# Routed attention and cosine-routed experts: one late block instead of two, a first wide item of 392 rooms placed right behind the early blocks and turned by TensorE, and the overflow branch moved into the last early result

## The chip, the cores and the metric

One core of a Trainium2 chip runs the whole program. The metric is the device time of one execution in microseconds (us); lower is better. The profile describes one execution by itself, measured from its first to its last instruction (the span).

## What is computed

An attention whose queries see only the keys of their own cluster is followed by a mixture of experts with one expert for each token. Cut to the part that the change touches:

```
def _moe_ref(x, expert_emb, tau, w1, w2):          # x: (3072, 512), E = 8, F = 1024
    ...
    expert_idx = np.argmax(logits, axis=1)         # one expert for each token
    ...
    for e in range(E):
        mask = expert_idx == e
        h = np.maximum(x[mask] @ w1[e], 0.0)       # w1[e]: 512 x 1024
        out[mask] = gate_w[mask, None] * (h @ w2[e])   # w2[e]: 1024 x 512
```

All of it is in float32. Which tokens go to which expert is known only while the program runs, so the kernel gives the experts rooms of fixed sizes and fills them.

## The kernel before

The first 330 us or so are the attention. They end in `x_rows`, a DRAM tensor with one row of 512 numbers for each token. After that the expert work is cut into *items*, each with an expert and a number of rooms for tokens. An item has a hidden stage (its rows times `w1`, then the positive part) and a result stage (times `w2`, then the gate), and its output rows are scattered to `out`. There are four kinds.

- Four *early* items of 128 rooms (`E0`), filled from the first half of the tokens while attention still runs.
- *Block* items of 128 rooms (`KX` of them, two before). They take what does not fit the wide items. The first block stood right behind the early items, the other is `last` at the very end.
- Eight *sized* items, called wide here, one for each expert, with the rooms of `CAPS`. The experts are ranked by what is left for them and get the rooms in that order. All but the smallest are multiplied by a scheme with seven products in place of eight: `sized_hidden` and `sized_result` cut rows and weights into quarters and call `seven`, which keeps partial sums. A wide item has 2 x 28 matmuls in its hidden stage and 56 in its result, each as wide as half its rooms. VectorE makes the sums of `x` (`x_sums`), of `w1` (`w1_sums`), of the hidden rows (`h_sums`) and of `w2` (`w2_sum`); ScalarE copies parts of `w2` (`w2_copy`). The smallest (200 rooms) uses `plain_hidden` and `plain_result`.
- *Whole* items of 128 rooms that stand inside `overflow()`, a branch (`tc.If`) taken only if more blocks are used than `KX`.

Five engines run their own lists, written out by hand (`tc.manual_schedule`), so the order of the calls in the code is the order on each engine. Weight loads, and the transfers of rows between DRAM and the chip's memory, are issued by SP in that order. GpSimd (POOL) issues the gathers of rows by index (`collect`) and the scatters to `out`. There are two buffers for `w1` (`w1s`) and two for `w2` (`w2s`). Wide items load their raw `w2` into one buffer (`slot2`), and their sums and copies fill the other one and some tiles beside it.

The rows of a block or wide item take a detour before: `collect` gathers them, `lay` writes them to the DRAM tensor `x_slots`, `bring` reads them back in another layout (`xs`, `xin`), and `turn_x` turns them on VectorE by 32 x 32 transposes into `xT`, with the model dimension on the partitions.

The order around the change was: hidden of the early item `E0[3]`, result of `E0[2]`, result of `E0[3]`, hidden of the first block, the matmuls that sort gates into slots (`pb.gates`), result of the block, the matmuls that spread these gates (`spread_gates`), and then the wide items from the largest to the smallest. The overflow branch stood between `plain_hidden` and `plain_result` of the last wide item. At the branch every engine loads the number of used blocks (`used`), compares and jumps. Where the paths meet, each engine waits for its own work: PE, VectorE and ScalarE for their instructions, POOL also for its transfers, SP for its own transfers. Later instructions that use a buffer which the branch could have used wait for the engine concerned to have come past that place.

Of the kernel before, what the change touches and what calls it, by code (L numbers as in the profile page):

```python
# [9 lines left out]
F32 = mybir.dt.float32  # L10
# [8 lines left out]
P = 128  # L19

SQ = 32
# [18 lines left out]
def kernel(  # L40
# [12 lines left out]
    nc = tc.nc  # L53
# [18 lines left out]

    CAPS = (344, 344, 336, 328, 280, 264, 248, 200)
    KX = 2
    assert len(CAPS) == E and max(CAPS) <= 512
# [6 lines left out]

    MORE = (2, 6, 12)
    NO = sum(MORE)
# [1134 lines left out]
    def collect(it):  # L1219

        to = mo.setdefault(it, {})["rows_in"] = []
        for i, (b, n) in enumerate(rows_of(it)):
            if it is sized[0]:
                x = szp.tile(
                    [P, FH, HC], F32, tag=("h11", "h12", "h21")[i], name="rows_in", bufs=1
                )
# [15 lines left out]
    def bring(it):  # L1242

        d = mo[it]
        if it.kind == "sized":
            to, n = szp.tile([P, max(WIDE), P], F32, tag="xs", name="xs", bufs=1), WIDE[it.j]
            d["xs"] = to
        else:
            to, n = xip.tile([P, NQ, P], F32, tag="xin", name="xin"), NQ
            d["xin"] = to  # L1250
        for w in range(NQ):
            nc.sync.dma_start(
                out=to[SQ * w : SQ * w + SQ, 0:n], in_=by_quads(x_slots, it, n)[w]
            )
# [26 lines left out]
    def turn_x(it, evict=None, xT=None):  # L1281
# [25 lines left out]
        evict(d["xT"], bk)  # L1307

    HC = max(CAPS) // 2
    KH = KD // 2  # L1310
# [41 lines left out]
    def w2_part(it, name):  # L1352

        parts = mo[it].setdefault("w2", {})
        if name not in parts:
            own = ("t2", "t4", "b21", "b22")
            if name in own:
                i = own.index(name)
                t = flat(w2s[0][:, 2 * i : 2 * i + 2]).rearrange("p (g f x) -> p g f x", g=2, f=FH)
# [40 lines left out]
    def seven(it, product, to, relu, then):  # L1400
# [6 lines left out]

        def saved(name, src):
            t = szp.tile([P, 2, HC], F32, tag=name, name=name, bufs=1)[:, :, 0:h]
            nc.scalar.copy(t, src)  # L1410
            return t
# [181 lines left out]
    def hidden(it, halves=(0, 1), span=(0, 512)):  # L1593

        d = mo[it]
        for half in halves:
            if half == 0 and span[0] == 0:
                d["hT"] = mop.tile([P, F], F32, tag="hT", name="hT")
            f0 = 512 * half
# [34 lines left out]

    def result(it, halves=(0, 1)):
        d = mo[it]
        for half in halves:
# [6 lines left out]
            bk = d["y_ps"]  # L1644
            for c in range(KF // 2 * half, KF // 2 * half + KF // 2):
                nc.tensor.matmul(  # L1646
# [5 lines left out]
                )  # L1652
            if half == 1:
                to = (sidxs[0] if it.kind == "early" else it.tables[2])[:, it.col : it.col + 1]
# [49 lines left out]
    YB = 1  # L1704
    kinds = 4 * "early " + "block " + E * "sized " + "block"
    items = []
    for i, kind in enumerate(kinds.split()):
        own = 1 if i > KA else i % 2
        items.append(Item(kind, sum(it.kind == kind for it in items), i % 2, own))
# [4 lines left out]
    later = items[KA:]  # L1714
    sized = later[1:-1]

# [69 lines left out]
    with tc.manual_schedule(engines=by_hand):  # L1786
# [96 lines left out]
        pb.experts()  # L1883
        weights1(later[0])
        result(E0[1], (0,))
# [9 lines left out]
        pb.token_rows(gidxs[1], sidxs[1])  # L1895
        collect(later[0])
        collect(sized[0])
# [18 lines left out]
        weights2(sized[0])  # L1916
        collect(sized[1])

        def overflow():
            n_used = nc.values_load(used[0:1, 0:1], min_val=0, max_val=KX + NO)  # L1920
            own = sized[-1]

            def more(j0, n):
                for j in range(j0, j0 + n):
                    it = Item("whole", KX + j, own.slot, own.slot2, more_tables)
                    it.col, it.gates, it.xin = j, more_gates, xin
# [8 lines left out]
            with tc.If(n_used > KX):  # L1935
# [3 lines left out]
                ]  # L1939
                xin = szp.tile([P, max(WIDE), P], F32, tag="xs", name="xs", bufs=1)[:, 0:NQ]  # L1940
                pb.hot_blocks(NB, NO)
# [22 lines left out]

# [66 lines left out]
        plain_hidden(it, steps)  # L2031
        overflow()
        weights2(last)
# [50 lines left out]
```

## Time and profile before

| | us |
|---|---|
| median of 3 runs (lowest to highest) | 658.21 (658.02 to 660.22) |
| the profiled execution's own time | 656.26 |
| its span, first to last instruction | 654.5 |
| PE busy in the span | 638.2 (98%) |
| VectorE (DVE) busy | 488.3 (75%) |
| ScalarE (ACT) busy | 315.4 (48%) |
| POOL busy | 177.6 (27%) |
| granted TensorE clock, mean | 0.996 |

PE is TensorE's matmul stream and PEld its weight loads, which lie beside it. In rows of the time line the columns are: start and duration in us from the span's start, engine, line of the kernel, operation, output<-input by the program's names, shape, and the number of equal instructions merged; in brackets stands the idle time of that engine just before, and what ended it. A float32 matmul stands as two records, so "x8" there is four matmuls of the code. A transpose by TensorE is one record.

### The profile page before, as it was taken

To read this page: it belongs to the slowest core of one execution; us is meant where nothing else is said; L and a number is where in the kernel's file an instruction comes from. 1 tells how busy PE (TensorE), PEld (TensorE's weight loads), DVE (VectorE), ACT (ScalarE), POOL (GpSimd) and SP (SyncE) were. 2 spreads that over 40 slices of the span, in tenths; PEclk is the share of its full clock that TensorE was granted. 3 is DMA by queue.
4 is the path that set the end of the run, shared out by engine and by line. 5 is a ranking of instruction groups with operands and counts; after the bars stand their busy time and mean duration, and the time that the engine had idled before them with its cause. 6 is when DMAs were issued, how large, how long until landed. Compare 5 with 4: busy or idle time off the path is not lost. (4 is left out here: it accounts for less than half of the span.)

```text
span 654.5 us, 16780 instructions
## 1 busy us (share of the span) xinstructions
PE 638.2 (98%) x6673; PEld 449.0 (69%) x6673; DVE 488.3 (75%) x806; ACT 315.4 (48%) x537; POOL 177.6 (27%) x382
## 2 busy tenths in 40 slices
PE   8999999999999999999999978999999999999996
PEld 4444444444444444445677655999999999999995
DVE  6988988998989999999768234677778778886220
ACT  6656655677655785667615201525252424434311
POOL 3222212312214112235756431220404040220211
PEclk9999999999999999999999989999999999999999
DMA  9855666777679778668989989886969687888753
GB/s 143 134 93 99 98 97 106 141 148 128 96 94 166 132 156 180 109 177 215 273 234 336 374 309 333 230 244 200 291 225 293 233 292 257 278 271 292 266 195 98
DMA packets 261537, 131.47 MB, mean 201 GB/s; under 512 B 208561, under 2 KB 229297, under 8 KB 261452
## 3 DMA queue, kind: packets, MB, share of 16 engines
q1 hardware_dynamic: 256876, 117.36, 71.2%
q0 software_dynamic: 4400, 12.92, 6.3%
q8 instruction: 54, 0.88, 0.6%
q14 instruction: 31, 0.25, 0.1%
q10 hardware_dynamic: 176, 0.05, 0.0%
HBM read 101.18 MB, written 23.54 MB: 191 GB/s over the span
## 5 line engine op out<-in xcount | busy, mean ns | idle before, releaser
L585 ACT ACTIVATE prob<-s_ps 128x768 f32<-128x768 f32 x192 | 154.3, 813 | 100.5 <-PE s_ps L574 98.8
L574 PE MATMUL s_ps<-qT,kT 64*64 64x384 f32 x1536 | 156.1, 483 | 0.0
L596 PE MATMUL o_ps<-prob,v 64*64 64x385 f32 x1536 | 141.2, 484 | 0.0
L615 DVE TENSOR_TENSOR acc<-acc,prob 128x768 f32<-128x768 f32 x128 | 121.4, 948 | 8.6
L596 PEld LDWEIGHTS o_ps<-prob,v 64*64 64x64 f32 x1536 | 57.4, 133 | 65.7 <-issue 58.1
L574 PEld LDWEIGHTS s_ps<-qT,kT 64*64 64x64 f32 x1536 | 55.1, 133 | 36.1 <-issue 31.9
L1141 POOL DMA_INDIRECT out_dram<-rows_out,sidx x22 | 22.9, 1039 | 158.9 <-DMA rows_out<-y_slots 154.9
L574 PE MATMUL s_ps<-hot 64*64 64x384 bf16 x768 | 64.4, 325 | 0.1
L574 PEld LDWEIGHTS <-hot 64*64 64x64 bf16 x768 | 23.9, 106 | 42.8 <-issue 40.6
L630 POOL COPY behind<-acc 1x1 f32<-1x1 f32 x30 | 6.7, 222 | 158.7 <-DVE acc L615 154.3
L1605 PEld LDWEIGHTS h_ps<-xTm,w1s 128*128 128x128 f32 x384 | 45.3, 198 | 6.4 <-issue 6.4
L1605 PE MATMUL h_ps<-xTm,w1s 128*128 128x128 f32 x384 | 46.0, 282 | 3.4 <-issue 3.4
L663 POOL COPY inv<-inv 32x12 f32<-32x12 f32 x128 | 33.0, 258 | 41.7 <-DVE inv L660 33.5
L1646 PE MATMUL y_ps<-w2s,hT 128*128 128x512 f32 x80 | 35.6, 595 | 4.4 <-DMA w2s<-in_moe_w_dram 4.4
L1130 POOL DMA_INDIRECT rows_in<-x_rows,gidx x24 | 29.0, 1207 | 21.5 <-DMA x_slots<-rows_in 16.3
L605 DVE SCALAR_TENSOR_TENSOR acc<-prob,prob 128x768 f32<-128x768 f32 x32 | 32.4, 1013 | 0.0
L1564 DVE STREAM_TRANSPOSE ys<-yT 128x352 f32<-128x352 f32 (+3 forms) x32 | 13.2, 469 | 23.2 <-ACT yT L1440 13.7
L1297 DVE STREAM_TRANSPOSE xTm<-xin 128x512 f32<-128x512 f32 x5 | 3.6, 711 | 36.2 <-DMA xin<-x_slots 19.1
L620 ACT COPY o_sb<-o_ps 128x770 f32<-128x770 f32 x32 | 25.6, 799 | 9.5 <-PE o_ps L596 9.5
L1646 PEld LDWEIGHTS y_ps<-w2s,hT 128*128 128x128 f32 x80 | 14.7, 190 | 21.6 <-issue 19.2
L632 POOL TENSOR_TENSOR o_sum<-o_sb 128x385 f32<-128x385 f32 x30 | 26.5, 884 | 1.4 <-ACT o_sb L620 0.9
L1410 ACT COPY u<-h_ps 128x344 f32<-128x344 f32 (+5 forms) x22 | 9.1, 413 | 33.4 <-PE h_ps L1503 21.6
(351 smaller groups left out, 1129.7 us busy)
## 6 DMA issues: line engine op xcount, KB each, us to landing
w1s<-in_moe_w_dram SPq DMA_DIRECT2D x12, 2048.0 KB, 9.4
w2s<-in_moe_w_dram SPq DMA_DIRECT2D x12, 2048.0 KB, 8.6
q<-in_q_dram SPq DMA_DIRECT2D x64, 96.0 KB, 4.1
k<-in_k_dram SPq DMA_DIRECT2D x64, 96.0 KB, 3.3
x_rows<-xb SPq DMA_DIRECT2D x64, 96.0 KB, 2.7
v<-in_v_dram SPq DMA_DIRECT2D x120, 48.0 KB, 2.0
xr<-x_rows SPq DMA_DIRECT2D x9, 512.0 KB
x_slots<-rows_in SPq DMA_DIRECT2D x17, 256.0 KB, 11.2
```

Source lines behind the costliest of these rows:

```text
L574: nc.tensor.matmul(s_ps[D * half : D * half + D, h, 0:HS], lhsT=l[rows, half], rhs=r[rows], start=part == (1 if len(parts) < 2 else 0), st ...
L585: nc.scalar.activation(d["prob"][:, :, 0:HS], d["s_ps"][:, :, 0:HS], ACTF.Exp, scale=scale)
L596: nc.tensor.matmul(g["o_ps"][D * h : D * h + D, half, 0:HE], lhsT=ld[n]["v"][keys, j, h], rhs=d["prob"][keys, h, 0:HE], start=(j == 0), st ...
L605: nc.vector.scalar_tensor_tensor(out=g["acc"], in0=un[i - 1]["prob"][:, :, 0:HS], scalar=NJ * EPS, in1=d["prob"][:, :, 0:HS], op0=ALU.add, ...
L615: nc.vector.tensor_tensor(g["acc"], g["acc"], d["prob"][:, :, 0:HS], ALU.add)
L620: nc.scalar.copy(t["o_sb"], g["o_ps"][:, :, 0:HE])
L632: add(t["o_sum"][:, hq], t["o_sb"][:, 0], t["o_sb"][:, 1], ALU.add)
L663: nc.gpsimd.tensor_copy(inv2[M * to : M * to + M, :, i % 2], inv[M * i : M * i + M])
L1130: nc.gpsimd.indirect_dma_start(out=to, out_offset=None, in_=of, in_offset=bass.IndirectOffsetOnAxis(ap=at, axis=0), bounds_check=n - 1, oo ...
L1141: inst = nc.gpsimd.indirect_dma_start(out=to, out_offset=bass.IndirectOffsetOnAxis(ap=at, axis=0), in_=of, in_offset=None, bounds_check=n - 1,
L1605: nc.tensor.matmul(bk[:, m : m + P], lhsT=w1s[it.slot][:, c, f0 + m : f0 + m + P], rhs=d["xT"][:, P * c : P * c + P], start=(c == 0), stop ...
L1646: nc.tensor.matmul(bk, lhsT=d["hT"][:, P * c : P * c + P], rhs=w2s[it.slot2][:, c], start=(c == 0), stop=(c == KF - 1),)
```

## The change

The rooms become 392, 344, 344, 336, 328, 280, 248, 200: the size 264 goes and 392 is new. One block is left (`last`). The first wide item comes right behind the early items. Its gathered rows no longer go through DRAM: `order_rows` copies them on VectorE into another order, `turn_rows` turns them by TensorE, and ScalarE and VectorE copy the turned rows to `xT`. The overflow branch stands between the second and third quarter of the result of `E0[3]`; all weight buffers swap their parity; the two saved tiles `u2` and `u3` share one buffer; a few tiles used by whole items are other ones.

```
-    CAPS = (344, 344, 336, 328, 280, 264, 248, 200)
-    KX = 2
+    CAPS = (392, 344, 344, 336, 328, 280, 248, 200)
+    KX = 1
...
-    MORE = (2, 6, 12)
+    MORE = (2, 6, 13)
...
+    def order_rows(it):
...
+            nc.vector.tensor_copy(
+                to.rearrange("p (c w i) -> p c w i", c=KD, w=NQ),
+                x.rearrange("p (w c i) -> p c w i", c=KD, w=NQ),
+            )
...
+    def turn_rows(it):
...
+            for c in range(KD):
+                nc.tensor.transpose(bk[:, c], x[:, P * c : P * c + P], ident[0:n, 0:n])
+            evict = nc.scalar.copy if i % 2 == 0 else nc.vector.tensor_copy
+            evict(d["xT"][:, :, P * i : P * i + n], bk)
...
         def saved(name, src):
+            name = "u2" if name == "u3" else name
...
-    def result(it, halves=(0, 1)):
+    def result(it, halves=(0, 1), parts=2):
...
-    kinds = 4 * "early " + "block " + E * "sized " + "block"
+    kinds = 4 * "early " + E * "sized " + "block"
...
-        own = 1 if i > KA else i % 2
+        own = 0 if i >= KA else i % 2
...
-        weights1(later[0])
+        weights1(sized[0])
...
-        collect(later[0])
         collect(sized[0])
...
-        weights1(sized[0])
-        lay(later[0])
-        lay(sized[0])
-        bring(later[0])
+        w1_sums(sized[0])
         result(E0[2])
-        weights2(later[0])
-        bring(sized[0])
-        turn_x(later[0])
-        w1_sums(sized[0])
-        turn_x(sized[0])
-        result(E0[3])
-        weights2(sized[0])
-        collect(sized[1])
+        order_rows(sized[0])
+        pb.gates(slot_gates)
...
-        first, last = later[0], later[-1]
-        hidden(first)
+        result(E0[3], (0, 1), 4)
+        overflow()
+        weights2(sized[0])
+        weights1(sized[1])
+        collect(sized[1])
+        lay(sized[1])
+        bring(sized[1])
+        result(E0[3], (2,), 4)
+        turn_rows(sized[0])
+        result(E0[3], (3,), 4)
+        spread_gates()
         x_sums(sized[0])
-        pb.gates(slot_gates)
-        lay(sized[1])
-        weights1(sized[1])
-        bring(sized[1])
-        result(first, (0,))
         w2_sum(sized[0], "t1")
-        result(first, (1,))
-        spread_gates()
...
         plain_hidden(it, steps)
-        overflow()
         weights2(last)
```

How the instructions stand on the engines shows where things went. First TensorE, before, from the hidden stage of `E0[3]` on (`w1s_59`, `w1s_58` and `w2s_60`, `w2s_61` are the two buffers of each weight; 48 rows of gates are left out at the first "...", 31 of their spreading at the second):

```order
L1605 MATMUL h_ps<-xTm,w1s_59 128x128 x32
L1646 MATMUL y_ps_5085<-w2s_60,hT 128x512 x8
L1646 MATMUL y_ps_5193<-w2s_61,hT 128x512 x8
L1605 MATMUL h_ps<-xTm,w1s_58 128x128 x32
L1072 LDWEIGHTS ohrb
...
L1646 MATMUL y_ps_5085<-w2s_60,hT 128x512 x8
L1578 LDWEIGHTS identb
...
L1467 MATMUL h_ps<-xTs,w1s_59 128x172 x4
```

And TensorE of the changed kernel at the same place, from the end of the gates on; what stands inside the branch is left out at the first "...":

```order
L1072 MATMUL misc_236<-rg24b,ohrb 128x72
L1686 MATMUL y_ps_5193<-w2s_61,hT 128x512 x4
L1950 TENSOR_LOAD used
L1965 COMPARE_AND_BRANCH
...
L1965 UNCONDITIONAL_BRANCH
L1686 MATMUL y_ps_5193<-w2s_61,hT 128x512 x2
L1340 MATMUL x_ps<-ident,ordered 128x128 x4
L1340 MATMUL h_ps<-ident,ordered 128x128 x8
L1340 MATMUL h_ps<-ident,ordered 128x32 x4
L1686 MATMUL y_ps_5193<-w2s_61,hT 128x512 x2
L1614 LDWEIGHTS identb
...
L1503 MATMUL h_ps<-xTs,w1s_58 128x196 x4
```

The 32 and 8 matmuls of the first block are gone; the gates moved ahead of the result of `E0[3]`, which is cut into pieces of four, two and two matmuls with the branch and 16 transposes between them, and the wide item follows at once.

SP, whose list is also the order in which the transfers are issued, before, from the weights of the first block on:

```order
L1180 DMA w1s_58<-in_moe_w_dram 128x4x1024
L1180 ISA
L1180 DMA w2s_61<-in_moe_w_dram 128x8x512
L1165 TENSOR_LOAD e_sized
L1165 ISA x2
...
L1180 DMA w1s_59<-in_moe_w_dram 128x4x1024
L1235 DMA x_slots<-rows_in 128x512 x3
L1235 DMA x_slots<-rows_in 96x512
L1252 DMA xin<-x_slots 32x4x128 x4
```

And SP of the changed kernel from there, with the inside of the branch left out:

```order
L1180 DMA w2s_61<-in_moe_w_dram 128x8x512
L1950 TENSOR_LOAD used
L1950 ISA x2
L1965 COMPARE_AND_BRANCH
...
L1965 UNCONDITIONAL_BRANCH
L1180 ISA
L1180 DMA w2s_60<-in_moe_w_dram 128x8x512
L1165 TENSOR_LOAD e_sized
...
L1180 DMA w1s_59<-in_moe_w_dram 128x4x1024
L1235 DMA x_slots<-rows_in 128x512 x2
```

The rows of the first wide item no longer pass through SP; its `w2` is the first transfer behind the branch, and `w1s_59`, `x_slots` there are of the second wide item.

More of the change, by code (lines that the diff above doesn't have):

```diff
@@ L1224, in collect @@
                 x = szp.tile(
-                    [P, FH, HC], F32, tag=("h11", "h12", "h21")[i], name="rows_in", bufs=1
+                    [P, FH, HC], F32, tag=("h11", "h12", "h21", "h22")[i], name="rows_in", bufs=1
                 )
@@ L1245, in bring @@
         if it.kind == "sized":
-            to, n = szp.tile([P, max(WIDE), P], F32, tag="xs", name="xs", bufs=1), WIDE[it.j]
+            to, n = szp.tile([P, max(WIDE[1:]), P], F32, tag="xs", name="xs", bufs=1), WIDE[it.j]
             d["xs"] = to
@@ L1307, in turn_x @@
         evict(d["xT"], bk)
+    def order_rows(it):
+        d = mo[it]
+        spare = szp.tile([P, max(WIDE), P], F32, tag="ys", name="ordered", bufs=YB)
+        spare = spare.rearrange("p u x -> p (u x)")
+        d["ordered"] = []
+        for i, (x, _) in enumerate(d.pop("rows_in")):
+            n = x.shape[0]
+            if DM * i + DM <= spare.shape[1]:
+                to = spare[0:n, DM * i : DM * i + DM]
+            else:
+                to = szp.tile([P, FH, HC], F32, tag="hS1", name="ordered", bufs=1)
+                to = to.rearrange("p f t -> p (f t)")[0:n, 0:DM]
+            nc.vector.tensor_copy(
+                to.rearrange("p (c w i) -> p c w i", c=KD, w=NQ),
+                x.rearrange("p (w c i) -> p c w i", c=KD, w=NQ),
+            )
+            d["ordered"].append(to)
+    def turn_rows(it):
+        d = mo[it]
+        d["xT"] = szp.tile([P, KD, SQ * max(WIDE)], F32, tag="xTs", name="xTs", bufs=1)
+        for i, x in enumerate(d.pop("ordered")):
+            n = x.shape[0]
+            if i == 0:
+                bk = psX.tile([P, DM], F32, tag="x_ps", name="x_ps")
+            else:
+                bk = psH.tile([P, 512], F32, tag="h_ps", name="h_ps")
+            bk = bk.rearrange("p (c t) -> p c t", c=KD)[:, :, 0:n]
+            for c in range(KD):
+                nc.tensor.transpose(bk[:, c], x[:, P * c : P * c + P], ident[0:n, 0:n])
+            evict = nc.scalar.copy if i % 2 == 0 else nc.vector.tensor_copy
+            evict(d["xT"][:, :, P * i : P * i + n], bk)
     HC = max(CAPS) // 2
@@ L1358, in w2_part @@
                 i = own.index(name)
-                t = flat(w2s[0][:, 2 * i : 2 * i + 2]).rearrange("p (g f x) -> p g f x", g=2, f=FH)
+                t = flat(w2s[1][:, 2 * i : 2 * i + 2]).rearrange("p (g f x) -> p g f x", g=2, f=FH)
             else:
@@ L1597, in hidden @@
             if half == 0 and span[0] == 0:
-                d["hT"] = mop.tile([P, F], F32, tag="hT", name="hT")
+                if it.kind == "whole":
+                    t = szp.tile([P, KD, SQ * max(WIDE)], F32, tag="yT", name="hT", bufs=1)
+                    d["hT"] = t.rearrange("p g t -> p (g t)")[:, 0:F]
+                else:
+                    d["hT"] = mop.tile([P, F], F32, tag="hT", name="hT")
             f0 = 512 * half
@@ L1644, in result @@
             bk = d["y_ps"]
-            for c in range(KF // 2 * half, KF // 2 * half + KF // 2):
+            for c in range(KF // parts * half, KF // parts * half + KF // parts):
                 nc.tensor.matmul(
@@ L1652, in result @@
                 )
-            if half == 1:
+            if half == parts - 1:
                 to = (sidxs[0] if it.kind == "early" else it.tables[2])[:, it.col : it.col + 1]
@@ L1714 @@
     later = items[KA:]
-    sized = later[1:-1]
+    sized, last = later[:-1], later[-1]
     def piece(n, name, *args):
@@ L1939, in overflow @@
                 ]
-                xin = szp.tile([P, max(WIDE), P], F32, tag="xs", name="xs", bufs=1)[:, 0:NQ]
+                xin = szp.tile([P, max(WIDE[1:]), P], F32, tag="xs", name="xs", bufs=1)[:, 0:NQ]
                 pb.hot_blocks(NB, NO)
```

4 lines of the change are left out of this document (2 added, 2 removed).

## The prediction

> **What bounds the kernel now.** I read the page's busy times first, then the time line of TensorE (PE) behind the attention, then who waits there.
>
> ```profile
> PE 638.2 (98%) x6673; PEld 449.0 (69%) x6673; DVE 488.3 (75%) x806; ACT 315.4 (48%) x537; POOL 177.6 (27%) x382
> 550.00:560.00 10.00, 10.00 (x87) 10.00 (x86) 9.79 (x15) 1.43 (x4) 3.58 (x5) 1.00 0.90 316
> ```
>
> PE is the bound: busy 98% of the span, and all 10 us of the second row, a stretch of 10 us inside the wide items where VectorE (third pair) is nearly full too. So an edit is worth what it takes off PE's line. PE's gaps lie where the early items hand over to the wide ones:
>
> ```profile
> 358.97 7.31 PE L1605 MATMUL h_ps<-xTm,w1s 128*128 128x128 f32 x64
> 366.11 7.03 PE L1646 MATMUL y_ps<-w2s,hT 128*128 128x512 f32 x16
> 374.69 7.10 PE L1646 MATMUL y_ps<-w2s,hT 128*128 128x512 f32 x16 [1.55 <-DMA w2s<-in_moe_w_dram]
> 385.22 9.01 PE L1605 MATMUL h_ps<-xTm,w1s 128*128 128x128 f32 x64 [3.42 <-issue]
> 394.07 0.94 PE L1072 MATMUL misc<-rg24b,ohrb 128*128 128x72 bf16 x24
> 397.87 7.10 PE L1646 MATMUL y_ps<-w2s,hT 128*128 128x512 f32 x16 [2.86 <-DMA w2s<-in_moe_w_dram]
> 405.33 0.30 PE L1578 MATMUL misc<-g3b,identb 128*32 128x66 bf16 x16 [0.36 <-DVE g3b L1082]
> 405.56 1.43 PE L1467 MATMUL h_ps<-xTs,w1s 128*128 128x172 f32 x8
> 406.83 1.33 PE L1467 MATMUL h_ps<-xS,w1s 128*128 128x172 f32 x8
> 408.00 1.33 PE L1467 MATMUL h_ps<-xS,t 128*128 128x172 f32 x8
> ```
>
> In order: hidden of `E0[3]`, result of `E0[2]`, result of `E0[3]`, hidden of the first block, gates, the block's result, spreading, and the first products of the first wide item. From 373.14 (366.11 + 7.03) to 405.56 are 32.42 us. Four gaps of 1.55, 3.42, 2.86 and 0.36 lie in them, and the block's hidden stage takes 9.01 where the same 64 records took 7.31. The long gap comes from the rows' way through DRAM:
>
> ```profile
> 384.40 0.71 DVE L1297 STREAM_TRANSPOSE xTm<-xin 128x512 f32<-128x512 f32 x1 [19.07 <-DMA xin<-x_slots]
> 401.42 1.76 DVE L1288 STREAM_TRANSPOSE xTs<-xs 128x512 f32<-128x512 f32 x3 [11.35 <-DMA xs<-x_slots]
> ```
>
> **The change, part by part.** I sum against the profiled execution (656.26 us by its own time, 654.5 in its span, so 1.76 around it). The median shown is 658.21, 1.95 above it; I take the sum off both.
>
> *The wide item of 392 for that of 264.*
>
> ```profile
> 561.05 1.06 PE L1467 MATMUL y_ps<-xTs,w1s 128*128 128x132 f32 x8
> 586.67 1.05 PE L1467 MATMUL h_ps<-xTs,w1s 128*128 128x124 f32 x8
> 627.06 1.52 PE L1545 MATMUL y_ps<-h,w2b 128*128 128x200 f32 x8
> 628.41 1.52 PE L1545 MATMUL y_ps<-h,w2s 128*128 128x200 f32 x8
> ```
>
> The item of 264 (132 columns) held PE from 561.05 to 586.67, 25.6 us. An item has 112 matmuls. At 172 columns four take 408.00 - 406.83 = 1.17, 0.292 each; at 200 columns 1.35, 0.338. Between them 196 gives 0.332 and the item 37.2 us: **+11.5**. The block's 40 matmuls go in the next part.
>
> *The stretch from 373.14 to the wide item.* What it holds afterwards:
> (a) Gates, 0.94, while the `w2` of `E0[3]` still lands. It was issued at 359.16 (row below) and landed by 374.69; one of the four row gathers beside it shrinks from 128 or 96 rows to 32, so I take 374.3: 1.2 us (bounds 0.9 and 1.6).
> (b) The result of `E0[3]`, in pieces: 7.1.
> (c) The branch, inside it.
>
> ```profile
> 612.22 10.99 PE L1527 MATMUL h_ps<-xTs,w1s 128*128 128x200 f32 x64
> 359.16 0.37 SPq L1180 DMA_DIRECT2D w2s<-in_moe_w_dram  x1
> 624.28 1.59 PE L1545 MATMUL y_ps<-h,w2b 128*128 128x200 f32 x8 [1.06 <-ACTq L1935]
> L1920 PEldq TENSOR_LOAD <-used x1: 487/487/487, 620.0 to 620.0; - x1
> L1935 PEldq COMPARE_BRANCH  x1: 3492/3492/3492, 620.6 to 620.6; - x1
> L1935 DVEq COMPARE_BRANCH  x1: 72/72/72, 614.9 to 614.9; - x1
> ```
>
> PE's jump took 3.49 us, and its sequencer got to it some 2.6 us before the last matmul ended (612.22 + 10.99), so 1.06 us of it showed as a gap. In the new place the sequencer can't run ahead by more than the four matmuls behind the wait for `w2` (3.5 us), less issuing them and the load of `used` (0.49): I estimate it at the jump by 375.6, past it by 379.2, while the array is done by 377.8. That is a gap of 1.4; bounds 0 (hidden) and 3.6 (wholly exposed). [...]
> (d) Sixteen transposes.
>
> ```profile
> L1304 PE MATMUL x_ps<-ident,rows x4: 272/273/328, 318.1 to 318.5; 128*128 128x128 f32 x4
> ```
>
> Four start within 0.4 us, some 0.11 apart: 1.8; the upper bound is 16 x 0.273 = 4.4. The copies of `order_rows` hide: VectorE idled for 19.07 us there, and the last rows had landed when SP sent them on, by 373.3:
>
> ```profile
> 368.45 4.83 SPq L1235 DMA_DIRECT2D x_slots<-rows_in  x4
> ```
>
> They end before 377. The copies to `xT` lie beside (b)'s last piece, 1.8 us.
> (e) Spreading, 0.3.
> (f) A new order on VectorE: the spread gates come ahead of `x_sums`.
>
> ```profile
> 403.22 0.52 DVE L1322 TENSOR_TENSOR xS<-xTs 128x344 f32<-128x344 f32 x1
> 407.57 0.64 DVE L1586 COPY parts<-misc 128x264 f32<-128x264 f32 x1
> 408.70 1.22 DVE L1384 TENSOR_TENSOR w2t<-w2s 128x1024 f32<-128x1024 f32 x1
> ```
>
> The gates take 408.70 - 407.57 = 1.13, the first sum 0.52 x 392/344 = 0.6; the second product needs it, and the first covers 4 x 0.332 = 1.3. With 0.2 for signals PE waits 0.6 (bounds 0 and 1.5).
> Together 1.2 + 7.1 + 1.4 + 1.8 + 0.3 + 0.6 = 12.4 in place of 32.42: **-20.0**. The half clock of the block's hidden stage and all four gaps go with it.
>
> *What is late next: the wide item's `w2`.* SP issues it behind the branch, into a buffer that the branch could have used, so not before PE is past it (379.3).
>
> ```profile
> DMA to landing us min/median/max: 8.3/8.6/9.8
> 407.38 1.05 ACT L1388 COPY w2b<-w2s 128x1024 f32<-128x1024 f32 x1
> ```
>
> That is the time to land of `w2` behind 400 us: 8.6, so 388.1. ScalarE's first copy of it stands between saving the first product (386.3) and the second (388.2), and the third bank is free only behind that. It ends at 389.2, the save at 389.6, and the fourth product would like to start at 389.6. **+0.4**; bounds 0 and 3 (landing in 9.8, with the gathers of the second wide item beside it, and a longer jump).
>
> *Other queues.* POOL meets the branch with a scatter in flight:
>
> ```profile
> 374.14 1.03 POOL L1141 DMA_INDIRECT out_dram<-y,sidx  x1 [7.25 <-ACT y L1657]
> L1935 POOLq COMPARE_BRANCH  x1: 58/58/58, 629.9 to 629.9; - x1
> L1935 POOLq INC_SWDGE_SEM  x1: 1508/1508/1508, 637.2 to 637.2; - x1
> ```
>
> It was held from 629.9 to 638.7 before, 8.8 us; from 375.9 that gives 384.7. Then come the gathers of the second wide item, `lay` and `bring`.
>
> ```profile
> 384.11 1.04 POOL L1130 DMA_INDIRECT rows_in<-x_rows,gidx  x1 [0.31 <-DMA xin<-x_slots]
> 408.38 2.00 SPq L1252 DMA_DIRECT2D xs<-x_slots  x4
> xs<-x_slots SPq DMA_DIRECT2D x12, 176.0 KB, 8.2
> ```
>
> Before, they took 24.3 us from the first gather to `bring`, with two weight loads queued between, and 8.2 to land. These loads now go first; taking one of them (8.6) off, the rows are there by 384.7 + 24.3 - 8.6 + 8.2 = 408.6. VectorE wants them behind the wide item's hidden stage (18.6 from 385.5), its first result product (2.7), four sums of 0.6 and four of 1.2 as above: about 414. Nothing shows, by 5 us.
>
> *`u2` and `u3` in one tile*: ScalarE's save of product 7 now waits for VectorE's sum from `u2`.
>
> ```profile
> 539.24 0.39 ACT L1410 COPY u<-h_ps 128x280 f32<-128x280 f32 x1 [0.69 <-PE h_ps L1467]
> 539.31 0.44 DVE L1427 TENSOR_TENSOR h<-h_ps,u 128x280 f32<-128x280 f32 x1
> ```
>
> This is the tightest of the 21 places: the sum ends at 539.75, so the save slips by 0.5, and one product in between (0.95) covers most of it. **+0.3**; bounds 0 and 1.
>
> *The branch gone from the end*: its 1.06 gap, **-1.1**; PE's last matmuls (below) and the scatter follow as they did.
>
> ```profile
> 642.32 7.11 PE L1623 MATMUL y_ps<-w2s,hT 128*128 128x384 f32 x32
> ```
>
> Sum: 11.5 - 20.0 + 0.4 + 0.3 - 1.1 = **-8.9 us**. Own time 656.26 - 8.9 = 647.4; from the median 658.21 - 8.9 = **649.3**.
>
> **The rivals.**
> *Forecast*, 649.3, own range 647.5 to 651. For it: PE full to 10.00 of 10 once the wide items run, so that its records are all that counts.
> *A new wait takes the old one's place*: the jump ends late, `w2` lands late, ScalarE holds the banks, or the second item's rows miss their 414. For it: each link starts from the one before, at transfer times that reach 9.8. Against: each is a microsecond or two. +3: 652.3.
> *The clock drops.* The block's 9.01 came behind a gap of 3.42, while the gap of 2.86 left the 7.10 behind it alone. If the jump is wholly exposed (3.6, or 2.2 more than I count), the same loss of 1.7 follows: +3.9, 653.2. [...]
> *Less is exposed*: jump hidden, no waits; -1.4 - 0.6 - 0.4 - 0.3 = 646.6.
> *Slower*: POOL at the branch. ScalarE's gating of the result of `E0[3]` reuses an output tile that the branch could scatter from, so it waits for POOL to have come past, and the banks of the wide item queue behind it on ScalarE. It has until 385; every microsecond beyond stops PE for one. POOL's 8.8 us give 384.7, so it just holds. To be slower by 0.5% POOL would have to hold until 397, 21 us at the branch, with the scatter's landing alone 12 us later than before; some 662. A small case of it is in the second rival.
> *The change doesn't do what it says*: if two blocks were used, the branch would run. By the reference's routing 462, 388, 339, 337, 325, 277, 241 and 191 tokens are left for the wide items. 388 fit into 392 with four to spare, as they did into 264 + 128; 462 need 336 + 126, as before, where the branch was skipped. I exclude it.
>
> **How the numbers follow.** Forecast 0.60, new wait 0.17, clock 0.08, less exposed 0.06, waits and clock together (within 0.5%, about 656) 0.05, slower 0.04. Half a per cent, 3.3 us, is about what a measurement of this kernel can tell from no change; faster starts below 654.9. The first four give 0.91 faster, then 0.05 and 0.04. The low end, 646.5, is the fourth case; the high end, 653.5, takes in the third. That leaves out the last two cases and the tails, under 0.2.
>
> **What would show it.** Right: wide item's first matmul at 385 (+-1.5) in PE's time line, its 112 matmuls at 0.332, no row gap on VectorE behind 384, PE without a gap between the plain item's stages, a gap of 1 to 2 us inside the result of `E0[3]`. Wrong: gaps with ScalarE as releaser among the first seven products (`w2` or POOL), half clock behind 378, or a wait of VectorE for `xs`.

## The result, and the profile after

| | before | after |
|---|---|---|
| median of 6 runs (lowest to highest), us | 659.22 (657.51 to 660.89) | 648.41 (648.14 to 649.09) |
| the profiled execution's own time | 656.26 | 648.23 |
| its span | 654.5 | 646.4 |

The ratio is 0.9836, with a 95% interval of 0.9815 to 0.9858: faster by 1.6%. The prediction was 649.3 with a range of 646.5 to 653.5. In the profiled spans the change is worth 8.1 us; the prediction's sum was 8.9. The medians are 10.8 apart because the runs of before lie 1 to 5 us above its one profiled execution, while those of after lie at it. What the other executions of before spent that time on was not traced; the 34 of them that ran beside the kernels below had a granted clock of 0.991 to 0.997, where the changed kernel ran at 0.997 to 1.0.

The page's busy times afterwards:

```profile
PE 635.8 (98%) x6609; PEld 450.9 (70%) x6609; DVE 494.3 (76%) x808; ACT 316.7 (49%) x536; POOL 177.1 (27%) x382
```

TensorE's time line afterwards, over the same stretch as before (columns as before; the last three rows are the start of the second wide item and of the two stages of the smallest one):

```profile
366.56 7.03 PE L1686 MATMUL y_ps<-w2s,hT 128*128 128x512 f32 x16
...
374.54 3.67 PE L1686 MATMUL y_ps<-w2s,hT 128*128 128x512 f32 x8 [0.17 <-SPq L1965]
379.09 1.96 PE L1686 MATMUL y_ps<-w2s,hT 128*128 128x512 f32 x4 [0.87 <-PEq L1965]
380.88 0.60 PE L1340 MATMUL x_ps<-ident,ordered 128*128 128x128 f32 x4
...
382.64 1.98 PE L1686 MATMUL y_ps<-w2s,hT 128*128 128x512 f32 x4
...
384.80 1.59 PE L1503 MATMUL h_ps<-xTs,w1s 128*128 128x196 f32 x8
386.88 1.56 PE L1503 MATMUL h_ps<-xS,w1s 128*128 128x196 f32 x8 [0.48 <-DVE xS L1357]
388.28 1.49 PE L1503 MATMUL h_ps<-xS,t 128*128 128x196 f32 x8
391.01 1.59 PE L1503 MATMUL h_ps<-xS,w1s 128*128 128x196 f32 x8 [1.24 <-ACT p L1446]
...
424.28 1.33 PE L1503 MATMUL y_ps<-xTs,w1s 128*128 128x172 f32 x8
...
605.50 11.00 PE L1563 MATMUL h_ps<-xTs,w1s 128*128 128x200 f32 x64
616.33 1.52 PE L1581 MATMUL y_ps<-h,w2b 128*128 128x200 f32 x8
```

The first wide product starts 11.21 behind the end of the result of `E0[2]` (384.80 - 373.59), where it took 32.42 before. The gaps of 1.55, 3.42 and 2.86 are gone, and so is the 1.06 between the last wide item's stages. In their place stand three smaller ones: 0.87 at the branch (released by PE's own queue at the branch's line), 0.48 for the first sum of `x`, 1.24 in front of the fourth product. That last one names ScalarE's save `p` as the releaser. ScalarE's time line tells why the save was late:

```profile
384.71 0.69 ACT L1697 ACTIVATE y<-y_ps,gatein 128x512 f32<-128x512 f32 x1 [1.74 <-PE y_ps L1686]
386.43 0.48 ACT L1446 COPY p<-h_ps 128x392 f32<-128x392 f32 x1 [1.03 <-PE h_ps L1503]
389.52 1.04 ACT L1423 COPY w2b<-w2s 128x1024 f32<-128x1024 f32 x1 [2.61 <-DMA w2s<-in_moe_w_dram]
390.48 0.48 ACT L1446 COPY p<-h_ps 128x392 f32<-128x392 f32 x1
```

The copy of `w2` stands in ScalarE's list ahead of the second save, and it waited for the load until 389.5. The load itself was issued late, behind the branch. The rows of the branch, and then of the load's issue (line, engine's queue, operation, count: least/median/most ns, first and last start in us):

```profile
L1965 POOLq COMPARE_BRANCH  x1: 58/58/58, 374.9 to 374.9; - x1
L1965 PEldq COMPARE_BRANCH  x1: 3752/3752/3752, 375.2 to 375.2; - x1
```

```profile
L1180 SPq DMA_DIRECT2D w2s<-in_moe_w_dram x1: 397/397/397, 379.1 to 379.1; - x1
```

So the new critical thread is: jump of TensorE until 378.95, `w2` issued at 379.1, landed at 389.5, copied, second save, bank free (the piece of memory that a product is written to), fourth product.

### The profile page after: what moved, and what is told of

Read it like the earlier page. It is cut to its first block, busy times and chain, and to the rows that moved or that the text cites. A ratio compares the mean times of both kernels' runs of the same rounds, so it can differ in the third digit from the quotient of the medians.

```text
span 646.4 us, 16585 instructions
## 1 busy us (share of the span) xinstructions
PE 635.8 (98%) x6609; PEld 450.9 (70%) x6609; DVE 494.3 (76%) x808; ACT 316.7 (49%) x536; POOL 177.1 (27%) x382
## 5 line engine op out<-in xcount | busy, mean ns | idle before, releaser
L1141 POOL DMA_INDIRECT out_dram<-rows_out,sidx x23 | 24.7, 1073 | 166.4 <-DMA rows_out<-y_slots 163.0
L1645 PEld LDWEIGHTS h_ps<-xTm,w1s 128*128 128x128 f32 x320 | 36.4, 192 | 2.2 <-issue 2.2
L1600 DVE STREAM_TRANSPOSE ys<-yT 128x352 f32<-128x352 f32 (+4 forms) x32 | 13.8, 486 | 30.5 <-ACT yT L1588 17.1
L1645 PE MATMUL h_ps<-xTm,w1s 128*128 128x128 f32 x320 | 37.0, 276 | 0.0
L1130 POOL DMA_INDIRECT rows_in<-x_rows,gidx x24 | 27.5, 1146 | 28.7 <-DMA x_slots<-rows_in 23.9
L1686 PE MATMUL y_ps<-w2s,hT 128*128 128x512 f32 x64 | 29.0, 598 | 1.0 <-PEq L1965 0.9
L1446 ACT COPY u<-y_ps 128x344 f32<-128x344 f32 (+5 forms) x20 | 8.6, 428 | 32.0 <-PE y_ps L1539 15.3
L1451 ACT ACTIVATE h<-h 128x344 f32<-128x344 f32 (+5 forms) x42 | 19.7, 475 | 4.5 <-DVE h L1468 2.6
```

The costliest lines, as they stand in the source:

```text
L1130: nc.gpsimd.indirect_dma_start(out=to, out_offset=None, in_=of, in_offset=bass.IndirectOffsetOnAxis(ap=at, axis=0), bounds_check=n - 1, oo ...
L1645: nc.tensor.matmul(bk[:, m : m + P], lhsT=w1s[it.slot][:, c, f0 + m : f0 + m + P], rhs=d["xT"][:, P * c : P * c + P], start=(c == 0), stop ...
L1686: nc.tensor.matmul(bk, lhsT=d["hT"][:, P * c : P * c + P], rhs=w2s[it.slot2][:, c], start=(c == 0), stop=(c == KF - 1),)
```

## Experiments

Each kernel is the changed one with the edit shown, timed in 5 rounds; "..." marks lines of the code that are left out. Spans are of one profiled execution. As executions do not all start the expert stage at the same time (the result of `E0[2]` starts between 365.7 and 368.5), distances are counted from the start of that result where it matters.

| label | median, us | ratio to before [95%] | span |
|---|---|---|---|
| (the change) | 648.41 | 0.9836 [0.9815, 0.9858] | 646.4 |
| after_again | 649.57 | 0.9875 [0.9854, 0.9896] | 648.2 |
| branch_end | 649.21 | 0.9851 [0.9815, 0.9887] | 647.5 |
| no_branch | 645.12 | 0.9794 [0.976, 0.9828] | 643.4 |
| copies_later | 647.71 | 0.9833 [0.9799, 0.9868] | 645.4 |
| branch_late | 653.75 | 0.9914 [0.988, 0.9947] | 650.5 |
| w1_later | 647.35 | 0.9842 [0.9821, 0.9863] | 645.1 |
| gathers_later | 647.45 | 0.9809 [0.9778, 0.984] | 645.4 |
| detour_nb | 651.06 | 0.9896 [0.9873, 0.9919] | 648.4 |
| two_blocks | 652.5 | 0.9913 [0.9888, 0.9939] | 651.2 |
| two_combo | 650.61 | 0.9856 [0.982, 0.9893] | 649.1 |
| combo_mid | 646.25 | 0.9796 [0.9765, 0.9828] | 643.1 |
| combo_late | 646.73 | 0.9798 [0.9767, 0.9829] | 645.0 |

### What the branch costs where it stands

```
         result(E0[3], (0, 1), 4)
-        overflow()
```

> The branch is left out: rows beyond the rooms would not be computed (with these inputs there are none). It prices the branch in its new place, with everything that hangs on it. My sums: 0.87 and 1.24 go, nothing comes back: span 644.3 (bounds 643.9 and 644.8). Rival: the jump lies beside other work but for its own gap, 645.5. If the branch cost as much as the prediction's bounds allow (3.6 and 3), the span would fall under 643.

Span 643.4, so 3.0 off, 0.9 more than my sum. TensorE's time line without the branch:

```profile
366.52 7.03 PE L1686 MATMUL y_ps<-w2s,hT 128*128 128x512 f32 x16
...
374.17 5.39 PE L1686 MATMUL y_ps<-w2s,hT 128*128 128x512 f32 x12
379.40 0.60 PE L1340 MATMUL x_ps<-ident,ordered 128*128 128x128 f32 x4
...
383.32 1.59 PE L1503 MATMUL h_ps<-xTs,w1s 128*128 128x196 f32 x8
385.35 1.57 PE L1503 MATMUL h_ps<-xS,w1s 128*128 128x196 f32 x8 [0.43 <-issue]
...
388.20 1.59 PE L1503 MATMUL h_ps<-xS,w1s 128*128 128x196 f32 x8
```

The fourth product starts 2.81 earlier than with the branch (388.20 for 391.01), at the same start of the result of `E0[2]`. I had added idle times only. Counted from start to start, a gap costs more than its idle time: the 0.87 is 1.11 (380.88 - 374.54 after, against 379.40 - 374.17 = 5.23 for the same matmuls here), and the 1.24 is 1.40 (391.01 - 388.28 against a pitch of 1.33 from product to product). The rest is 0.37 ahead of the result of `E0[3]`.

Back at the end, with the rest of the change kept (the whole items take that place's buffers again):

```
-        overflow()
...
         plain_hidden(it, steps)
+        overflow()
```

> The overflow branch goes back between the last wide item's two stages, everything else of the change stays. My sums: the gap of 0.87 inside the result of E0[3] goes, and with it the 1.24 in front of the wide item's fourth product, since SP then issues the wide item's w2 as soon as the result of E0[2] is done (373.6) and it lands by about 383, before its first copy; the 1.06 between the last item's stages comes back. Span 646.4 - 0.87 - 1.24 + 1.06 = 645.3 (bounds 645.0 and 646.0). Rival: taking the branch off the end was a gain of its own, as the prediction counted it, and the 1.24 is ScalarE's own business and not the load's; then the 1.24 stays, only the 0.87 is exchanged for 1.06, and the span is 646.6 or more.

My number missed. The 0.87 went, but three things did not come out as I said. The copy of `w2`, the return of the gap at the end, and one late instruction, each from the time line of its engine (two rows of ScalarE, then two of TensorE) in this kernel:

```profile
387.34 1.04 ACT L1423 COPY w2b<-w2s 128x1024 f32<-128x1024 f32 x1 [1.88 <-DMA w2s<-in_moe_w_dram]
579.48 0.40 ACT L1476 ACTIVATE yT<-y_ps 128x280 f32<-128x280 f32 x1 [4.84 <-PE h_ps L1503]
```

```profile
574.06 3.98 PE L1539 MATMUL y_ps<-h,w2s 128*128 128x140 f32 x32
617.36 1.59 PE L1581 MATMUL y_ps<-h,w2b 128*128 128x200 f32 x8 [1.63 <-PEq L1961]
```

`w2` was issued at 373.6, 5.5 earlier, and landed at 387.3, only 2.2 earlier: it took 13.7, with the other `w1` and the row gathers behind it. So the gap in front of the fourth product fell from 1.24 to 0.56 and did not go. The jump at the end showed a gap of 1.63 (1.06 in before). And ScalarE ran an instruction at 579.48 whose matmuls had ended at 578.04 (574.06 + 3.98), which cost 1.4; the last section comes back to it. The fastest of the five runs had a span of 645.3, what I had summed, the slowest 648.3. So the medians do not show that either place of the branch is better, and leaving it out is worth 3 us in the new place.

One step the other way, behind the third quarter:

```
-        result(E0[3], (0, 1), 4)
+        result(E0[3], (0, 1, 2), 4)
         overflow()
...
-        result(E0[3], (2,), 4)
         turn_rows(sized[0])
```

> The branch moves behind the third quarter of the result of E0[3]: six matmuls of the code stand between the wait for its w2 and the branch, 5.5 us in place of 3.67. My theory: TensorE's sequencer runs ahead over all six and meets the branch at the same time, so the gap of 0.87 goes; but w2 of the wide item is issued no earlier, the products start 0.87 earlier and the wait for the copy grows from 1.24 to 2.1. Span unchanged, 646.4 (bounds 646.0 and 646.8). Rival 1: each gap counts by itself: 645.5. Rival 2: the sequencer can't run ahead over six; then jump and load come up to 1.8 later and the span is up to 648.2.

The span came out above all three. TensorE's time line, and its queue at the branch:

```profile
374.22 5.39 PE L1686 MATMUL y_ps<-w2s,hT 128*128 128x512 f32 x12 [0.62 <-SPq L1965]
379.91 0.63 PE L1340 MATMUL x_ps<-ident,ordered 128*128 128x128 f32 x4 [0.30 <-PEq L1965]
...
392.33 1.97 PE L1503 MATMUL h_ps<-xS,w1s 128*128 128x196 f32 x8 [3.58 <-ACT p L1446]
394.09 2.82 PE L1503 MATMUL h_ps<-xTs,t 128*128 128x196 f32 x8
```

```profile
L1965 PEldq COMPARE_BRANCH  x1: 3952/3952/3952, 374.9 to 374.9; - x1
L1965 PEldq EVENT_SEMAPHORE  x1: 51/51/51, 379.7 to 379.7; - x1
```

The sequencer did run ahead over all six matmuls: the jump began at 374.9 and ended at 378.85. But it signalled that it was past the branch only at 379.7, when those matmuls had ended (374.22 + 5.39 = 379.61). `w2` was issued then, landed at 390.9, and TensorE stood for 3.58. Behind that gap a product took 2.82 where it takes 1.49: the clock was halved (granted clock 0.68 from 392 to 396). The span holds a start 0.8 earlier and a late instruction of 1.0 on ScalarE as well, which about cancel. That is the prediction's second and third rival at once, some 4 to 5 us, and it was one quarter of a result away.

### Why the first wide item's `w2` was late

SP's load of the next item's `w1` moved out of its way:

```
-        weights1(sized[1])
         collect(sized[1])
         lay(sized[1])
+        weights1(sized[1])
```

> SP issues w1 of the second wide item behind that item's rows (lay) and not right behind w2 of the first. The prediction took 8.6 for that w2 to land and it took 10.4. My theory: w1, issued 1.3 behind it, shares the transfer; without it w2 lands 8 to 8.6 behind its issue, by 387.6, the copy ends before the second product does, and the 1.24 goes: span 645.2 (bounds 644.8 and 645.6; one late instruction on ScalarE would add 1). Rival 1: the row gathers and the scatter slow it, w1 does not: 10 and more again, span 646.4. Rival 2: w1 now delays bring, VectorE waits for xs near 413 and the span grows, up to 650.

Rival 1. The load's issue and the copy that waits for it, in this kernel:

```profile
L1180 SPq DMA_DIRECT2D w2s<-in_moe_w_dram x1: 398/398/398, 377.9 to 377.9; - x1
```

```profile
388.19 1.04 ACT L1423 COPY w2b<-w2s 128x1024 f32<-128x1024 f32 x1 [2.43 <-DMA w2s<-in_moe_w_dram]
```

It took 10.3 again, and the gap was 1.14, so the span inside the theory's bounds is luck: this execution ran 0.8 earlier from the start on, and the gap at its jump was 0.57 in place of 0.87. All five runs of this kernel (646.9 to 647.6) do lie below the five of the repeat of the change that were timed beside them (649.1 to 650.2); whether an earlier start is the reason in each of them was not traced. Then the row gathers instead:

```
-        collect(sized[1])
-        lay(sized[1])
-        bring(sized[1])
         result(E0[3], (2,), 4)
         turn_rows(sized[0])
         result(E0[3], (3,), 4)
+        collect(sized[1])
+        lay(sized[1])
+        bring(sized[1])
```

> POOL's three row gathers of the second wide item (and SP's transfers of them) move behind the scatter of E0[3]. w2 of the first wide item took 10.3 to 10.4 to land with them beside it, with or without the second w1. My theory: they are what slows it; alone it takes 8.6 or less, lands by 387.7, and the 1.24 falls to 0.3 or less: span 645.3 (bounds 645 and 646.2). Rival 1: the transfer takes 10 there in any company, 646.4. Rival 2: the rows of the second item now come too late (VectorE turned them at 413.5): VectorE waits for xs and the span grows to 648 or more.

The load's issue, then ScalarE's and TensorE's time lines in this kernel:

```profile
L1180 SPq DMA_DIRECT2D w2s<-in_moe_w_dram x1: 397/397/397, 378.8 to 378.8; - x1
```

```profile
387.29 1.05 ACT L1423 COPY w2b<-w2s 128x1024 f32<-128x1024 f32 x1 [0.66 <-DMA w2s<-in_moe_w_dram]
```

```profile
378.80 1.95 PE L1686 MATMUL y_ps<-w2s,hT 128*128 128x512 f32 x4 [1.29 <-PEq L1965]
...
387.90 1.49 PE L1503 MATMUL h_ps<-xS,t 128*128 128x196 f32 x8
389.23 1.49 PE L1503 MATMUL h_ps<-xS,w1s 128*128 128x196 f32 x8
```

8.5 to land, no gap in front of the fourth product: the gathers, or the first transfers of their rows, which moved with them, were what slowed it. The wait for `xs` that rival 2 feared did not come. The span shows little of it, since this execution's jump was longer (gap 1.29) and it had a late instruction on ScalarE too, by 0.9.

The other way is to need `w2` later. ScalarE's first copy behind the third save, for the first item only:

```
-                    w2_copy(it, "b11")
+                    if k:
+                        w2_copy(it, "b11")
...
                     w2_copy(it, "b22")
+                    if not k:
+                        w2_copy(it, "b11")
```

> Only for the first wide item, ScalarE's first copy of w2 moves from behind the save of the first product to behind that of the third. My theory: the 1.24 in front of the fourth product is that copy, waiting for w2 until 389.5 while the saves queue behind it; the saves then come right behind their products and the 1.24 goes: span 645.2 (bounds 645.0 and 645.6). Rival 1: the bank is held by something else (the w2 sums on VectorE stand ahead of the sum that frees the bank of the fourth product, and they wait for the same load): the gap moves to a later product and the span stays at 646.4. Rival 2: two copies in a row hold the save of the fifth product: a gap of up to 1 there, span 646.2.

The gap of 1.24 went, as the theory said; a piece of rival 1 came. TensorE's and VectorE's time lines:

```profile
388.51 1.49 PE L1503 MATMUL h_ps<-xS,w1s 128*128 128x196 f32 x8
...
392.90 1.59 PE L1503 MATMUL h_ps<-xTs,t 128*128 128x196 f32 x8 [0.25 <-ACT u L1446]
```

```profile
389.44 2.36 DVE L1419 TENSOR_TENSOR w2t<-w2s 128x1024 f32<-128x1024 f32 x2 [2.25 <-DMA w2s<-in_moe_w_dram]
391.71 0.56 DVE L1463 TENSOR_TENSOR h<-h_ps,u 128x392 f32<-128x392 f32 x1
```

VectorE's two sums of `w2` stand ahead of the sum that reads `u2`, and the save of `u3` goes into the same tile, so it waited: 0.25. The span fell by 1.0 only, with an early start of 0.8 in it, because here too an instruction on ScalarE came 1.0 late at 579.

### Both together

```
         result(E0[3], (3,), 4)
+        x_sums(sized[0])
         spread_gates()
-        x_sums(sized[0])
-        w2_sum(sized[0], "t1")
...
+                elif i == 3 and not k:
+                    w2_sum(it, "t1")
+                elif i == 4 and not k:
+                    w2_sum(it, "t3")
+                    w2_copy(it, "b11")
+                elif i == 5 and not k:
+                    w2_copy(it, "b22")
```

For the first item these stand in place of the earlier copies and sums of `first_steps`.

> For the first wide item everything that reads its w2 moves back: ScalarE's copies from behind the first and third product to behind the fifth and sixth, VectorE's two sums from ahead of the sum that frees u2 to behind it; and the first sums of x go ahead of the spread gates. The branch stays. My theory: 1.24 and most of the 0.48 go and nothing new comes, since w2 is now needed at 392: from 1.72 down to 0.2 of gaps among the first seven products, span 644.8 (bounds 644.3 and 645.5, with up to 1 more where the early stages ran late, as the repeats showed). Rival: saves and copies crowd ScalarE in the second half of the hidden stage and a gap of about 1 comes up there: 645.8.

```profile
383.55 1.59 PE L1503 MATMUL h_ps<-xTs,w1s 128*128 128x196 f32 x8
...
387.63 1.49 PE L1503 MATMUL h_ps<-xS,w1s 128*128 128x196 f32 x8
...
420.80 1.33 PE L1503 MATMUL y_ps<-xTs,w1s 128*128 128x172 f32 x8
```

No gap is left in the item: TensorE's time line has it from 383.55 to 420.80, 37.25 in place of 39.48. The span, 643.1, lies below my bounds, but 0.8 of that is an earlier start and 0.3 a shorter jump (gap 0.54 for 0.87). The median is 646.25, the ratio to before the lowest of the kernels that keep the branch. It was not timed side by side with the change, and its interval (0.9765 to 0.9828) just touches that of the change (0.9815 to 0.9858); by the rows it is 2.2 us faster.

With that cover the branch behind the third quarter should have paid, so the edits of this kernel and of the one that moved the branch were put together:

> The same, with the branch behind the third quarter. In the kernel that moved the branch alone, TensorE came past it only at 379.7, when its six matmuls had ended, w2 was issued with it, and the wait for w2 grew from 1.24 to 3.58 and halved the clock. My theory: it was only the lateness of w2 that cost; with 2 us of cover for it the smaller gap at the branch (0.30 for 0.87) is all that is left: span 644.3 (bounds 643.8 and 645). Rival: w2 lands at 391 to 392, the sums on VectorE come late and hold u2 or the result's first products: 646 or more.

It did not: 646.73 against 646.25, timed side by side, span 645.0. The halved clock is gone (the fourth and fifth product take 1.49 each, for 1.97 and 2.82 with the branch moved alone), so the lateness of `w2` was what had cost there. The first product came no earlier behind the start of the result of `E0[2]` (17.9 for 17.8), and `w2` landed late enough for ScalarE's copies to hold a save in the second half of the hidden stage, as the rival had it in kind:

```profile
396.60 1.59 PE L1503 MATMUL y_ps<-xS,t 128*128 128x196 f32 x8 [0.40 <-ACT p L1446]
```

Of the 1.9 in the spans, 0.3 is a later start and about 1.0 a late instruction on ScalarE.

### Where the gain comes from

The rows of the first wide item through DRAM again, with the branch left out to keep it out of the way:

```
+        lay(sized[0])
+        bring(sized[0])
         result(E0[2])
-        order_rows(sized[0])
...
-        turn_rows(sized[0])
+        turn_x(sized[0])
```

> To be set beside the kernel without the branch (span 643.4): the branch is left out here too (rows beyond the rooms would not be computed), and the first wide item's rows go through DRAM and VectorE as before, in place of TensorE's turn. My theory: the last rows land by 373.5, 2.5 to write them, 8.2 to read them back, 2.4 to turn them (four of 0.59): first product at 386.7 and not 383.3, behind a gap of some 5 on TensorE that also halves the clock for a few us (1.5). w2 is issued behind the rows and lands by 389 or later: up to 3 more. Span 648.3 (bounds 646 and 652). Rival: with nothing queued between, the rows come in time, and TensorE has 1.8 less to do: 641.6 to 643.4.

Against the kernel without the branch: span 648.4 for 643.4, as the theory had it (648.3). Its 2.5 for writing the rows was an estimate that no row shows by itself; 373.5 + 2.5 + 8.2 puts them back on the chip at 384.2, and VectorE got them at 385.07. TensorE's time line, and the row of VectorE that its first product waited for:

```profile
374.25 7.11 PE L1690 MATMUL y_ps<-w2s,hT 128*128 128x512 f32 x16 [0.26 <-DMA w2s<-in_moe_w_dram]
...
386.48 2.95 PE L1507 MATMUL h_ps<-xTs,w1s 128*128 128x196 f32 x8 [4.88 <-issue]
389.22 2.82 PE L1507 MATMUL h_ps<-xS,w1s 128*128 128x196 f32 x8
```

```profile
385.07 2.09 DVE L1292 STREAM_TRANSPOSE xTs<-xs 128x512 f32<-128x512 f32 x4 [10.23 <-DMA xs<-x_slots]
```

A gap of 4.88 for rows that came late from `x_slots`, and two products at half clock behind it (2.95 and 2.82 for 1.49; granted clock 0.50 from 386 to 390). The turn by TensorE is worth 5.0 us by the spans and 5.9 by the medians, which were not timed side by side.

The sizes of before, in the order of the change, with both blocks at the end (the second one's loads, rows and stages stand behind the first's):

```
-    CAPS = (392, 344, 344, 336, 328, 280, 248, 200)
-    KX = 1
+    CAPS = (344, 344, 336, 328, 280, 264, 248, 200)
+    KX = 2
```

> The sizes of before (344, 344, 336, 328, 280, 264, 248, 200 and two blocks) in the order of the change: wide items right behind the early ones, rows turned by TensorE, branch in the same place, both blocks at the end. It parts the trade of rooms from the closed gaps. By the prediction's terms: 11.5 less for the wide items (264 for 392), 14.2 more for a second block at full clock, 0.5 more for w2, since shorter products end earlier: span 646.4 + 3.2 = 649.6 (bounds 648.5 and 651.5). So of the 8.1 in the spans about 5 would be order, turning and branch, and 3 the trade. Rival: the trade is all of the gain, the gaps come back elsewhere: 654 or more. Second rival: the shorter items give ScalarE and VectorE no cover and new gaps come up among the products: 652.

Within my bounds by the span, but not for my reason. The shorter products reached the fourth one earlier, so the wait grew to 3.45 and the clock was halved behind it (granted clock 0.57 from 391 to 395):

```profile
391.06 2.37 PE L1503 MATMUL h_ps<-xS,w1s 128*128 128x172 f32 x8 [3.45 <-ACT p L1446]
393.23 2.12 PE L1503 MATMUL h_ps<-xTs,t 128*128 128x172 f32 x8
```

So it was run again with the edits that take the wait away:

> The sizes of before in the order of the change, with the two edits of the first kernel of this call, so that the wait of 3.45 and the half clock behind it, which that size mix had, are gone. It leaves the trade of rooms alone: 14.2 for a second block less 11.5 for the larger item, so 2.7 over the first kernel of this call: span 647.5 (bounds 646.8 and 648.5). Rival: a second block at the end costs more than its matmuls (its rows or weights come late there): 649 or more; or the mix of 651.2 was slow for another reason than the wait: 650.

649.1, outside my bounds: 6.0 over its partner in span and 4.4 in the medians, more than the 2.7 of the trade. The blocks at the end cost just their matmuls, without a gap (14.0 for the first, from 615.79 to 629.81). The excess is in gaps elsewhere: 0.51 in the first item, 0.84, 0.71 and 0.49 in the items of 264 and 248, behind late instructions on ScalarE, and a longer jump (gap 0.99 for 0.54). By these terms the trade is 2.4 (14.0 less 11.6 for the larger item). The runs differ by 4.4 to 6.0, and whether the other gaps belong to that mix of sizes or to the one execution stays open.

### The spread

> The changed kernel as it is, beside the others of this call, to set its spread against theirs. My theory: what differs between its runs are single late instructions on ScalarE of about 1 us (in one trace of a variant one ran 1.44 after the matmuls it waited for), not the clock: runs between 648 and 650, median 648.5, granted clock 0.998 or more. Rival: the gaps sometimes halve the clock: then some runs show 0.996 or less and lie 2 us higher.

Runs from 649.08 to 650.19, 1.2 above the first median; granted clock 0.997 to 1.0, and no run 2 us above the others, so the clock is not what spreads them. But the profiled one had none of ScalarE's late instructions; it stood 1.45 at 357.18, in the early items, until POOL had finished a bookkeeping copy. So part of a microsecond or two between executions arises ahead of everything that was changed. Against the runs of before beside it the repeat is worth 8.0 (657.57 - 649.57), or 1.2%.

## Why the prediction was right, by its own steps

| step | predicted | measured |
|---|---|---|
| stretch to the first wide product, without the wait for the sum | -20.6 | -21.2 |
| wide item of 392 for that of 264 | +11.5 | +11.6 (37.25 without gaps, less 25.62) |
| wait for the first sum of `x` | +0.6 | +0.75 |
| `w2` late | +0.4 | +1.4 |
| shared tile of `u2`, `u3` | +0.3 | +0.2 |
| branch gone from the end | -1.1 | -1.2 |
| early part of this execution | 0 | +0.45 |
| sum | -8.9 | -8.0 |

Waits are counted here from start to start. The last matmul ended at 649.43 before (642.32 + 7.11) and at 641.41 after, 8.0 earlier; the span's 8.1 agrees.

That the median came out within a microsecond of the forecast is in part luck. By the rows the change is worth 0.9 less than the sum. But the forecast also carried over the 1.95 by which the median of before lay above its profiled execution, and afterwards the median lies only 0.2 above its own (648.41 for 648.23). The two errors have opposite signs; the first alone would have given 650.2, still inside the range.

Of the signs of being right that the prediction named, all came, but the gap inside the result of `E0[3]` was 0.87 where it said 1 to 2. One sign of being wrong came too: the 1.24 in front of the fourth product has ScalarE as releaser. It belongs to the mis-sized term below.

*The stretch.* Gates and wait for `w2` of `E0[3]`, 1.0 of 1.2; transposes 1.76 of 1.8; the gap at the branch 0.87 of 1.4. The estimate that only the four matmuls behind the wait for `w2` stand between the sequencer and the branch gave 375.6 to 379.2 for the jump; it ran from 375.2 to 378.95. The step took the jump as about as long as in the old place (3.49, beside 0.07 on VectorE), and that held: in all the new places the jump took 3.39 to 4.17 us on TensorE. What it spends that time on is not shown. The 0.2 for signals in the wait for the first sum was an estimate that no row of before shows; afterwards the waiting product started 0.15 behind the end of that sum (386.88, for VectorE's 386.17 + 0.56).

*The late `w2` is the term that was mis-sized*: +0.4 in the sum, 1.4 measured. The step "landing in 8.6" took the duration of loads deep in the wide items. Here three row gathers run beside the load; it took 10.4, and 8.5 in the one trace where they were moved. The 0.4 itself does not follow from the step's own times, which have the save done at 389.6, just when the product was due. The bounds of 0 to 3 held, and the chain of the step (issue at 379.1, ScalarE's copy ahead of the save, third bank) is what the rows show.

*POOL.* The slower rival let it stand 8.8 at the branch, until 384.7. It stood from 374.9 to 379.9:

```profile
374.60 1.02 POOL L1141 DMA_INDIRECT out_dram<-y,sidx  x1 [6.51 <-ACT y L1697]
379.86 0.18 POOL L1126 COPY rest<-rest 1x1 f32<-1x1 f32 x1 [4.24 <-DMA out_dram<-y,sidx]
```

ScalarE's gating ran at 384.71 as soon as its matmuls had ended, so this rival had 5 us more room than I gave it. The second item's rows were in time, as expected: VectorE turned them without a wait.

```profile
413.46 1.76 DVE L1288 STREAM_TRANSPOSE xTs<-xs 128x512 f32<-128x512 f32 x3
```

*The shared tile.* This term was not tried by itself; its gap of 0.22 or 0.23 stands in the item of 280 that the step named, in every trace.

*The rivals.* The new wait stayed small here (1.24) and the clock was not halved (granted 1.00 from 391 to 395), but moving the branch by one quarter brought both, a wait of 3.58 and a granted clock of 0.68 behind it, at 653.75, between the 653.2 of the clock alone and the 656 of both together.

## What to carry to other kernels

A branch whose body is not run still cost TensorE its jump, 3.39 to 4.17 us in these traces, and in this program it ended for the others only when the matmuls issued ahead of it were done (with the branch behind the third quarter they ended at 379.6 and the signal came at 379.7). What waits for it is late by the whole of that, here a weight load that was issued at 379.1 and at 373.6 with the branch elsewhere. So have its first reader stand well back, as the kernel with both edits does; starting the load ahead of the branch was not tried. Price a transfer by what runs beside it at its new place (10.4 to land here, 8.5 with the row gathers moved away), not by its median elsewhere (8.6). And count a wait from start to start: here that added some 0.2 to each idle time.

## What was not expected of the hardware

- The length of the jump on TensorE differs from trace to trace, from 3.39 to 4.17 us, and the gap behind it goes with it (0.54 and 1.29). Two executions of the one kernel that was traced twice had 3.75 and 3.81, so whether the edits or the single execution set it is not shown.
- At one place, ScalarE's last instruction for the result of the sixth wide item, it started 0.9 to 1.8 us after the matmuls that it reads had ended, in six of thirteen traces; in the others within 0.04. Its cause is open. From the first to the eighth product of the next item it made 7.4 to 8.3 us of 6.55. Some 0.5 of that stands in front of the seventh, in all six, released by the save into the shared tile. By the rows of `branch_end` the late instruction makes VectorE's work late (it turns the rows at 579.92, behind an idle 3.02 with ScalarE as releaser), its sum from `u2` too (583.92 to 584.33), and the save of `u3` waits for that (584.42); so the shared tile has a price there as well. One of the six traces had two more late instructions elsewhere, of 1.3 and 2.2.
- Four gaps of 3.42 to 4.88 us on TensorE halved its clock for the products behind them, and one of 2.86 did not; the granted clock was 0.50 to 0.68 over the four microseconds from the end of the four, and 1.00 behind the 2.86. What a gap between 2.86 and 3.42 does is not shown.
- `w2` issued 5.5 earlier landed only 2.2 to 2.8 earlier (13.7 and 13.1 for 10.4), with the same loads and gathers behind it.
